# Attention scores as half-height products from the queries as loaded, instead of full-height products from zero-padded queries

## The chip, the cores and the metric

The kernel runs on one core of one Trainium2 chip. The metric is the time of the whole program on the device in microseconds. Three runs of the kernel before took 835.89, 838.58 and 844.72 us; their median, 838.58 us, is the time before. One further execution was profiled, and every row below comes from it.

## The reference

Block-sparse attention over 4 batches, 8 heads, 768 positions and 64 dimensions, followed by a two-layer network with an erf gate.

```python
scores = scale * np.matmul(q, k.transpose(0, 1, 3, 2))     # q, k: (4, 8, 768, 64), scale = 1/8
# blocks of 32 positions, 24 of them. Query block i sees key block j where
#   |i - j| <= 1, or i or j is block 0 or 23, or j is one of i's 3 sampled blocks
scores = np.where(mask, scores, -1e9)
attn = softmax(scores); x = attn @ v                        # x: 3072 tokens of 512
h = x @ w_in                                                # 512 -> 2048
g = h * erf(softplus(h))
out = g @ w_out                                             # 2048 -> 512
```

## The kernel before

Heads are paired: a pair's two heads lie in the two halves of the 128 partitions, 64 dimensions each, so queries and keys of a pair fill all partitions. A batch has 16 units of attention work. Ten are middle units ("m"): 5 tiles t of four query blocks, each in two quads of four heads (two pairs). Six treat the last tile, blocks 21, 22, 23 and 0: four "f" units, one for each pair, for the two blocks that see every key, and two "e" units for blocks 21 and 22.

A middle unit's four query blocks need 256 key columns each: 96 of the window (tile `kx`), 96 of the sampled blocks (gathered by GpSimd into `kg`, four buffers, one for each query block) and 64 of the two end blocks (`kx` again). `scores` (L565) writes them to one PSUM tile `s` of 128 x 1024 float32, of which there is one buffer. Before the change the stationary operand is `qm` (L131): 64 columns for each block of a pair, the first 32 with head 0's queries and zeros in head 1's partitions, the last 32 the other way round. One product of full height so gives both heads' scores, and a unit has 2 pairs x 3 parts x 4 blocks = 24 products of 128 rows by 64 columns. Two blocks go to the two halves of the output partitions. The products are in float32. An f unit is two products of 128 x 128 with 512 and 256 moving columns, an e unit 12 of 128 x 64.

`order_q` (L146) fills `qm` from the loaded tile `qt` by two copies of 64 partitions x 512, on VectorE save for two tiles of the first batch (ScalarE). `load_q` (L134) loads `qt`. `next_queries` (L804), called in a step after `soft_max`, does `order_q` of the next tile and `load_q` of the one after on every second unit, so that the load waits for the copy, and the copy for the scores that still read `qm`.

The main loop (L978) has a step for each of 96 groups of the network, and two more. A step issues, in this order for TensorE: `ff_first` (24 products, tile `h`), `values` of the attention unit begun two units earlier (tile `po`), `scores` of a new unit where the list `until` gives the step one, and `ff_second` (12 products, tile `o`) of the group two steps back. The queues of VectorE, ScalarE and SyncE follow the same written order; every engine keeps program order. SyncE issues the loads, the gathers of values `vb<-vtab`, the stores and the transposes of `p` to `pT`; a wait at its head holds all behind it. After `scores` come `soft_max` and `soft_low` (VectorE), `soft_exp` (ScalarE) and `soft_turn` (a DMA transpose). Ahead of the loop four middle units and the splitting of the weights are written out by hand; there TensorE does the transposes.

Of the kernel before, what the change touches and what calls it, by code (L numbers as in the profile page):

```python
# [9 lines left out]
F32 = mybir.dt.float32  # L10
# [8 lines left out]
P = 128  # L19
BLOCK = 32  # L20
# [22 lines left out]
def sparse_attention_moe(ctx: ExitStack, tc: tile.TileContext, qT, kT, v, sampled, w_in, w_out, out):  # L43
# [22 lines left out]
    pe, act, dve, pool, sp = (InOrder(e) for e in (nc.tensor, nc.scalar, nc.vector, nc.gpsimd, nc.sync))  # L66
# [61 lines left out]


    qts = {}  # L130
    qm = cp.tile([P, HP, 4, 2, BLOCK], F32, tag="qm", name="qm")  # L131
    pool.memset(qm, 0.0)

    def load_q(b, t):  # L134
        place, tag, bufs = (mo, "g", FF_LAG + 1) if b == 0 and t in (1, 2) else (ld, "qt", 1)
        qt = place.tile([P, HP, P], F32, tag=tag, name=f"qt_{b}_{t}", bufs=bufs)
        rows = qT[b].rearrange("(r t) d s -> (t d) r s", t=2)
        if t < MT:
            c = (1 + 4 * t) * BLOCK
            sp.dma_start(qt, rows[:, :, c : c + P])  # L140
        else:
            sp.dma_start(qt[:, :, : 3 * BLOCK], rows[:, :, S - 3 * BLOCK :])
            sp.dma_start(qt[:, :, 3 * BLOCK :], rows[:, :, :BLOCK])
        qts[b, t] = qt

    def order_q(b, t):  # L146
        qt = qts.pop((b, t)).rearrange("p r (j c) -> p r j c", c=BLOCK)
        copy = act.copy if b == 0 and t in (1, 2) else dve.tensor_copy
        for a in range(2):
            copy(qm[a * D : (a + 1) * D, :, :, a, :], qt[a * D : (a + 1) * D])  # L150

    QW = 4 * VW
    vb = cp.tile([P, VGS, 2, 2 * QW], F16, tag="vb", name="vb")
# [400 lines left out]
    def key_columns(b, i, rows, pr):  # L554

        kx, kg = kxs[b], kgs[b, i]
        return (
            (0, 96, kx[rows, i - 1 : i + 2, pr, :]),
            (96, 192, kg[rows, :, pr, :]),
            (192, 256, kx[rows, 0 : NB : NB - 1, pr, :]),  # L560
        )
# [3 lines left out]
    def scores(unit):  # L565
        kind, b, n = unit[0], unit[1], unit[2:]
        tag = "_".join(str(x) for x in unit)
        s = ps_s.tile([P, 1024], F32, tag="s", name=f"s_{tag}")
        if kind == "m":

            t, quad = n
            s4 = s.rearrange("p (h r w) -> p h r w", h=2, r=2)
            for r in range(2):
                pr = 2 * quad + r
                for part in range(3):
                    for j in range(4):
                        o = slice((j % 2) * 64, (j % 2) * 64 + 64)
                        q_ = qm[:, pr, j].rearrange("p a c -> p (a c)")
                        c, e, keys = key_columns(b, 1 + 4 * t + j, slice(0, P), pr)[part]
                        pe.matmul(s4[o, j // 2, r, c:e], q_, keys, start=True, stop=True)  # L580
            softs[unit] = (s, 4, 256)
        elif kind == "e":
            (quad,) = n
            s3 = s.rearrange("p (r w) -> p r w", r=HP)
            for r in range(2):
                for part in range(3):
                    for j in range(2):
                        o = slice(j * 64, j * 64 + 64)
                        q_ = qm[:, 2 * quad + r, j].rearrange("p a c -> p (a c)")
                        c, e, keys = key_columns(b, NB - 3 + j, slice(0, P), 2 * quad + r)[part]  # L590
                        pe.matmul(s3[o, r, c:e], q_, keys, start=True, stop=True)
            softs[unit] = (s[:, :512], 2, 256)
        else:
            (pr,) = n
            q_ = qm[:, pr, 2:].rearrange("p n a c -> p (n a c)")
            for c, e in ((0, 512), (512, S)):
                keys = kxs[b][:, c // BLOCK : e // BLOCK, pr, :]
                pe.matmul(s[:, c:e], q_, keys, start=True, stop=True)
            softs[unit] = (s[:, :S], 1, S)

    xTs = {}
# [3 lines left out]
    def values(b, t, quad):  # L605
        po = ps_po.tile([P, 4, D + 1], F32, tag="po", name=f"po_{b}_{t}_{quad}")
        for hl in range(4):
            r, a = divmod(hl, 2)
            pr = 2 * quad + r
            c = quad * QW + hl * VW  # L610

            todo = [[] for _ in range(4)]
            for x, ln in ((0, 0), (0, 1), (1, 0)):
                for half in range(2):
                    for j in range(4):
                        if t < MT:
                            pT = pts["m", b, t, quad][:, ((j // 2) * 2 + r) * 4 + x * 2 + half]
                            col = (j % 2) * 64 + a * 32
                            vg = vb[:, slot_of[b, 1 + 4 * t + j]]
                        elif j in (1, 2):  # L620
                            pT, col = pts["e", b, quad][:, r * 4 + x * 2 + half], (j - 1) * 64 + a * 32
                            vg = vb[:, slot_of[b, NB - 4 + j]]
                        else:
                            continue
                        w = slice(c, c + D + 1) if ln == 0 else slice(c + D + 2, c + VW)
                        todo[j].append((pT[:, col : col + 32], vg[:, half, w]))
                if t == MT:
                    for k in range(KT):
                        for j in (0, 3):
                            pT, col = pts["f", b, pr][:, x * KT + k], (0 if j else 64) + a * 32  # L630
                            w = slice(c, c + D + 1) if ln == 0 else slice(c + D + 2, c + VW)
                            todo[j].append((pT[:, col : col + 32], vb[:, slot_of[b, -1 - k // 2], k % 2, w]))
            for m in range(max(len(x) for x in todo)):
                for j in range(4):
                    if m < len(todo[j]):
                        lhs, rhs = todo[j][m]
                        w = rhs.shape[1]
                        pe.matmul(
                            po[j * 32 : j * 32 + 32, hl, :w], lhs, rhs, start=m == 0, stop=m == len(todo[j]) - 1
                        )  # L640
        pos[b, t, quad] = po
# [162 lines left out]
    def next_queries(m):  # L804

        b, n = divmod(m, per)
        if n < 10 and n % 2 == 1:
            order_q(b, n // 2 + 1)
            if n < 9:
                load_q(b, n // 2 + 2)  # L810
        if n == per - 1 and b + 1 < B:
            order_q(b + 1, 0)
            load_q(b + 1, 1)

    def behind(m):

        b, n = divmod(m, per)
        if b + 1 < B:
            c = b + 1
            if n == 10:  # L820
                load_q(c, 0)
            k = n if b else 2 * (n - 10) if n > 9 else -1
            if k in ((1, 3, 5, 7) if b else (2, 4, 6, 8)):
                order_k(c, (k - 1) // 2)
            if k in (0, 2, 4, 6):
                load_k(c, k // 2)
            if k == 8:
                have_k.add(c)
            if b == 0:
                n -= 4  # L830
            if n in (1, 7):
                load_v(c, 0)
            if n == 3:
                load_v(c, 1)
            if n in (2, 4):
                square_v(c, n // 2 - 1)
            if n == 5:
                scale_v(c)
            if n in (5, 6):
                split_v(c, 1, n - 5)  # L840
            if n in (8, 9):
                split_v(c, 0, n - 8)
            if n == 9:
                have_v.add(c)
# [9 lines left out]
    def used_keys(unit):  # L854
        nonlocal kfree
        if unit[0] == "m" and unit[3] == 1:
            kfree += 4
        elif unit[0] == "e" and unit[2] == 1:
            kfree += 4
# [21 lines left out]
    for i in range(4):  # L881
        load_weight(sp, "i", i)
    load_q(0, 1)
    load_q(0, 2)
    for n in range(3):
        place_v(0, *divmod(n, 2))
    for b in range(B):
# [3 lines left out]
    for pr in range(HP):  # L891
        order_k(0, pr)
    place_v(0, 1, 1)
    order_q(0, 0)
    have_k.add(0)
    gathers(0)
    numbers[0] = block_numbers(1, 5, SYNC)
# [18 lines left out]

    scores(units[1])
    used_keys(units[1])
    gathers(0)
    for i in range(10, 16):  # L920
        load_weight(pool, "i", i)
# [1 line left out]
    work("Di1")  # L923
    soft_max(units[1])
    soft_exp(units[1])
    order_q(0, 1)
    work("Qi1 Di2 Qi2 Di3 Qi3")
    soft_low(units[1])

# [8 lines left out]
    soft_turn(units[2])  # L938
    scores(units[3])
    used_keys(units[3])  # L940
    work("Qi6 Di7 Qi7 Do0")
    set_apart()
    soft_max(units[3])
# [10 lines left out]
    norm(*seen(units[1]))  # L954
    work("Hi0")
    turn(*seen(units[1]))
    order_q(0, 2)
    soft_low(units[3])
    values_of(seen(units[2]))
    work("Li0 Hi1")  # L960
# [6 lines left out]
    turn(*seen(units[3]))  # L967
    work("Do2")
    gathers(0)
    load_q(0, 3)  # L970
    begun = FIRST

    on_pe[0] = False
# [4 lines left out]
    for m in range(len(groups) + FF_LAG):  # L978
# [23 lines left out]
        if unit:  # L1002
            scores(unit)
            used_keys(unit)
        if last:
            ff_gate(*last)
        if place:
# [5 lines left out]
                ff_second(*groups[m - FF_LAG], u)  # L1013
        if unit:
            soft_max(unit)
            next_queries(begun - 1)
        if group:
            ff_power(*group)
        if unit:
# [54 lines left out]
```

## Time and profile before

| | us |
|---|---|
| median of 3 runs | 838.58 |
| profiled execution | 838.56 |
| its span from first to last instruction | 836.8 |
| TensorE matmul busy (PE) | 710.8 (85%) |
| weight loads (PEld) | 504.8 (60%) |
| VectorE (DVE) | 554.4 (66%) |
| ScalarE (ACT) | 601.1 (72%) |
| GpSimd (POOL) | 123.7 (15%) |
| chain that ended last: PE h, PE o, PE s_m, PE po | 18%, 18%, 5%, 3% of the span |
| mean granted clock of TensorE, share of full | 0.944 |

The profiled execution lies 1.8 us over its span and within 0.1 us of the median. Busy time of TensorE counts the tail of each product too; products overlap in it, so counts and starts say more than busy time. A float32 product appears in the trace as two weight loads and two matmuls, a float16 one as one of each. In a shape such as `128*64 128x96 f32`, 128*64 are the rows and columns of the stationary operand and 96 the moving columns.

### The profile page before, as it was taken

Reading aid. Unit: us, or ns where it says so; the run is one execution under the profiler, and the core shown is the slowest. Engines: PE = TensorE matmul, PEld = TensorE weight load, DVE = VectorE, ACT = ScalarE, POOL = GpSimd, SP = SyncE. Lnnn points to the kernel's source line nnn. Section 1 sums busy time; section 2 is a strip of 40 time slices with the busy share of each in tenths; the row PEclk is TensorE's granted clock in tenths of the full one; section 3 lists DMA queues with packets and bytes.
Section 4 is the critical chain, followed back from the end, with each engine's and each line's share of the span. In section 5 each row is a group of like instructions: output and inputs, shape, how many; then the busy total and the mean of one; then the engine's idle time right before and its main releaser. Section 6 shows DMA issues by size and latency. Waiting matters only on the chain.

```text
span 836.8 us, 26712 instructions
## 1 busy us (share of the span) xinstructions
PE 710.8 (85%) x11100; PEld 504.8 (60%) x11100; DVE 554.4 (66%) x977; ACT 601.1 (72%) x999; POOL 123.7 (15%) x344
## 2 busy tenths in 40 slices
PE   1253637899897899899999899999999899999997
PEld 1252424566665667566777666667777576766664
DVE  3994796887764766766566676756677567654454
ACT  4654657987865766887768778868678678776774
POOL 5430111001222220100201231000111100000000
PEclk9775867989998999999999999999999999999999
DMA  8999953687899697661497886633576758211000
GB/s 325 297 257 318 243 120 90 164 207 164 172 212 209 178 205 198 186 131 45 136 216 178 210 198 192 167 79 83 117 167 166 190 103 188 53 33 40 1 27 26
DMA packets 199930, 131.61 MB, mean 157 GB/s; under 512 B 144000, under 2 KB 167168, under 8 KB 199808
## 3 DMA queue, kind: packets, MB, share of 16 engines
q1 hardware_dynamic: 196384, 118.10, 58.1%
q0 software_dynamic: 3424, 11.80, 4.3%
q8 instruction: 87, 1.43, 0.7%
q14 instruction: 35, 0.29, 0.1%
HBM read 83.88 MB, written 12.95 MB: 116 GB/s over the span
## 4 chain that ended last, share of the span: by engine, by line
PE 47%; DVE 15%; issue 12%; ACT 10%; DMA 10%; SPq 2%; POOL 2%; POOLq 1%; ACTq 0%
PE h L59 18%; PE o L59 18%; PE s_m L59 5%; DMA vb<-vtab 4%; PE po L59 3%; DVE g L59 2%; ACT pf_m L59 2%; DVE q L59 2%; DVE mx_m L59 2%; DMA vtab<-vn 2%; SPq L59 2%; ACT x L59 2%; DVE p_m L59 2%; POOL kg L59 2%; ACT q L59 2%
## 5 line engine op out<-in xcount | busy, mean ns | idle before, releaser
L59 PE MATMUL h<-xT,wi 128*128 128x256 f16 x2304 | 274.2, 276 | 14.9 <-ACT wi L59 7.5
L59 PE MATMUL o<-wo,g 128*128 128x512 f16 x1152 | 270.3, 385 | 7.9 <-DVE wo L59 4.0
L59 PEld LDWEIGHTS <-wi 128*128 128x128 f16 x2304 | 227.4, 99 | 65.5 <-ACT wi L59 8.8
L59 PEld LDWEIGHTS <-g 128*128 128x128 f16 x1152 | 110.3, 99 | 133.0 <-issue 14.8
L59 ACT ACTIVATE x<-x 128x512 f32<-128x512 f32 x288 | 181.5, 630 | 9.1
L59 POOL COPY kg<-kx 128x128 f32 x264 | 90.5, 394 | 286.2 <-PE s_m L59 183.6
L59 ACT ACTIVATE pf_m<-s_m,nb_m 128x256 f32<-128x256 f32 x160 | 62.7, 475 | 65.4 <-DVE nb_m L59 59.5
L59 DVE SCALAR_TENSOR_TENSOR q<-x,q 128x512 f32<-128x512 f32 x96 | 66.7, 695 | 61.4 <-ACT x L59 60.1
L59 ACT ACTIVATE x<-h,isg 128x512 f32<-128x512 f32 x96 | 65.2, 680 | 36.3 <-PE h L59 35.7
L59 PE MATMUL s_m<-kx,qm 128*64 128x64 f32 (+1 forms) x1280 | 75.0, 249 | 6.8 <-ACT pf_m L59 4.2
L59 ACT ACTIVATE q<-q 128x512 f32<-128x512 f32 x96 | 59.5, 620 | 29.6 <-DVE q L59 29.6
L59 DVE SCALAR_TENSOR_TENSOR q<-q,h 128x512 f32<-128x512 f32 x96 | 65.5, 682 | 22.6 <-ACT q L59 22.6
L59 DVE TENSOR_TENSOR p_m<-pf_m,p_m 128x1024 f16<-128x1024 f32 x40 | 49.3, 1232 | 32.3 <-ACT p_m L59 32.3
L59 DVE SCALAR_TENSOR_TENSOR g<-q,g 128x512 f16<-128x512 f32 x96 | 67.0, 698 | 3.3
L59 PE MATMUL po<-vb,pT_m 128*32 128x65 f16 (+1 forms) x3840 | 44.7, 201 | 25.7 <-DMA vb<-vtab 15.0
L59 PEld LDWEIGHTS s_m<-kx,qm 128*64 128x64 f32 x1280 | 59.7, 146 | 10.4 <-ACT pf_m L59 4.9
L59 ACT ACTIVATE q<-x 128x512 f32<-128x512 f32 x96 | 60.5, 630 | 3.1
L59 DVE TENSOR_REDUCE mx_m<-s_m 128x4 f32<-128x1024 f32 x40 | 48.8, 1219 | 20.2 <-PE s_m L59 20.2
L59 PEld LDWEIGHTS <-pT_m 128*32 128x32 f16 x3840 | 38.0, 97 | 36.8 <-DMA vb<-vtab 16.3
L59 PE MATMUL s_m<-kg,qm 128*64 128x96 f32 x640 | 46.9, 261 | 3.2 <-POOL kg L59 2.2
L59 DVE TENSOR_TENSOR x<-xf,x 128x512 f16<-128x512 f32 x24 | 16.9, 703 | 43.3 <-ACT x L59 43.3
L59 DVE TENSOR_SCALAR g<-q 128x512 f16<-128x512 f32 x96 | 41.3, 431 | 3.3
(115 smaller groups left out, 623.7 us busy)
## 6 DMA issues: line engine op xcount, KB each, us to landing
vb<-vtab SPq DMA_DIRECT2D x280, 65.0 KB, 2.9
vb<-vtab SPq DMA_DIRECT2D x32, 390.0 KB, 4.1
vraw<-in_v_dram SPq DMA_DIRECT2D x10, 768.0 KB, 5.1
vtab<-vn SPq DMA_DIRECT2D x16, 390.0 KB, 5.4
vb<-vtab SPq DMA_DIRECT2D x12, 520.0 KB, 5.0
qt<-in_qT_dram SPq DMA_DIRECT2D x20, 256.0 KB, 3.3
out_dram<-wo SPq DMA_DIRECT2D x20, 256.0 KB, 4.3
vb<-vtab SPq DMA_DIRECT2D x36, 130.0 KB, 3.0
```

The costliest lines, as they stand in the source:

```text
L59: done = call(*args, **kwargs)
```

## The change

`qm`, its clearing and `order_q` are gone. `qt` has two buffers and stays until its scores are done; the products take their stationary operand from it, with 64 rows, one head at a time. A middle unit has 4 products of 64 rows x 128 columns for the end blocks (all four query blocks of a head at once, 64 moving columns), then 32 of 64 rows x 32 columns with 96 moving columns. In `s` the head's half of the tile is now the outer index: head a writes columns 512a to 512a+511, the query block j partitions 32j to 32j+31. An e unit has 24 products of 64 x 32, an f unit four of 64 x 64; in these two the heads' outputs share columns and differ in partitions. `values` reads `pT` at the new places. `next_queries` only loads, and is called right after `scores`.

```diff
-    qm = cp.tile([P, HP, 4, 2, BLOCK], F32, tag="qm", name="qm")
-    pool.memset(qm, 0.0)
     def load_q(b, t):
-        place, tag, bufs = (mo, "g", FF_LAG + 1) if b == 0 and t in (1, 2) else (ld, "qt", 1)
-        qt = place.tile([P, HP, P], F32, tag=tag, name=f"qt_{b}_{t}", bufs=bufs)
+        qt = ld.tile([P, HP, P], F32, tag="qt", name=f"qt_{b}_{t}", bufs=2)
...
-    def order_q(b, t):
-        qt = qts.pop((b, t)).rearrange("p r (j c) -> p r j c", c=BLOCK)
-        copy = act.copy if b == 0 and t in (1, 2) else dve.tensor_copy
-        for a in range(2):
-            copy(qm[a * D : (a + 1) * D, :, :, a, :], qt[a * D : (a + 1) * D])
...
             t, quad = n
-            s4 = s.rearrange("p (h r w) -> p h r w", h=2, r=2)
+            qt = qts[b, t]
+            s4 = s.rearrange("p (a r w) -> p a r w", a=2, r=2)
+            for pr, r, a in ((2 * quad + n // 2, n // 2, n % 2) for n in range(4)):
+                rows = slice(a * D, (a + 1) * D)
+                pe.matmul(s4[:, a, r, 192:], qt[rows, pr], kxs[b][rows, 0 : NB : NB - 1, pr, :], start=True, stop=True)
+            for r in range(2):
+                pr = 2 * quad + r
+                for part in range(2):
+                    for j in range(4):
+                        o = slice(j * BLOCK, (j + 1) * BLOCK)
+                        for a in range(2):
+                            rows = slice(a * D, (a + 1) * D)
+                            c, e, keys = key_columns(b, 1 + 4 * t + j, rows, pr)[part]
+                            pe.matmul(s4[o, a, r, c:e], qt[rows, pr, o], keys, start=True, stop=True)
...
-                    for j in range(2):
-                        o = slice(j * 64, j * 64 + 64)
-                        q_ = qm[:, 2 * quad + r, j].rearrange("p a c -> p (a c)")
-                        c, e, keys = key_columns(b, NB - 3 + j, slice(0, P), 2 * quad + r)[part]
-                        pe.matmul(s3[o, r, c:e], q_, keys, start=True, stop=True)
+                    for j in range(2):
+                        for a in range(2):
+                            rows, o = slice(a * D, (a + 1) * D), j * 64 + a * BLOCK
+                            c, e, keys = key_columns(b, NB - 3 + j, rows, pr)[part]
+                            q_ = qt[rows, pr, j * BLOCK : (j + 1) * BLOCK]
+                            pe.matmul(s3[o : o + BLOCK, r, c:e], q_, keys, start=True, stop=True)
...
-            q_ = qm[:, pr, 2:].rearrange("p n a c -> p (n a c)")
             for c, e in ((0, 512), (512, S)):
-                keys = kxs[b][:, c // BLOCK : e // BLOCK, pr, :]
-                pe.matmul(s[:, c:e], q_, keys, start=True, stop=True)
+                for a in range(2):
+                    rows = slice(a * D, (a + 1) * D)
+                    keys = kxs[b][rows, c // BLOCK : e // BLOCK, pr, :]
+                    pe.matmul(s[a * 64 : a * 64 + 64, c:e], qts[b, MT][rows, pr, 64:], keys, start=True, stop=True)
...
     def next_queries(m):
-        if n < 10 and n % 2 == 1:
-            order_q(b, n // 2 + 1)
-            if n < 9:
-                load_q(b, n // 2 + 2)
-        if n == per - 1 and b + 1 < B:
-            order_q(b + 1, 0)
-            load_q(b + 1, 1)
+        if n in (1, 3, 5, 7):
+            load_q(b, n // 2 + 2)
+        elif n in (9, 15) and b + 1 < B:
+            load_q(b + 1, n // 15)
...
         if unit:
             scores(unit)
             used_keys(unit)
+            next_queries(begun - 1)
...
         if unit:
             soft_max(unit)
-            next_queries(begun - 1)
```

The code by hand ahead of the loop loses its three `order_q` and the early `load_q(0, 2)` and `load_q(0, 3)`, and gets `next_queries(1)` and `next_queries(3)` after the scores of units 1 and 3.

## Rows read from the trace of the kernel before

**Rows 1.** Windows by stage: start:end, length, busy us per engine (instructions), PEclk, DMA share, GB/s.

```profile
0.00:95.00 95.00, 37.62 (x746) 31.57 (x747) 63.06 (x104) 49.74 (x82) 31.93 (x78) 0.77 0.95 292
95.00:180.00 85.00, 56.76 (x1040) 38.78 (x1037) 70.82 (x110) 67.30 (x110) 11.39 (x34) 0.82 0.59 148
180.00:300.00 120.00, 104.47 (x1791) 74.65 (x1791) 79.14 (x145) 85.63 (x148) 24.41 (x65) 0.96 0.86 194
300.00:460.00 160.00, 154.10 (x2501) 110.60 (x2488) 105.88 (x192) 121.95 (x206) 21.97 (x63) 1.00 0.67 158
...
500.00:640.00 140.00, 134.61 (x2157) 96.38 (x2156) 93.92 (x172) 107.62 (x180) 17.06 (x55) 1.00 0.58 140
640.00:700.00 60.00, 56.46 (x958) 40.92 (x956) 39.28 (x73) 42.65 (x73) 5.27 (x18) 0.97 0.69 158
...
597.78:611.28 13.50, 13.50 (x225) 9.78 (x217) 9.55 (x18) 9.60 (x17) 0.00 (x0) 1.00 0.69 140
```

**Rows 2.** The chain of waits from 597 to 625: start us, us, what.

```profile
597.85 1.94 PE s_m L59 x48
599.79 2.70 PE o L59 x12
602.49 2.62 PE h L59 x24
605.11 2.59 PE o L59 x12
607.70 2.62 PE h L59 x24
610.32 1.04 PE po L59 x95
```

**Rows 3.** The chain, 355 to 375: an f unit; then timelines of PE matmuls.

```profile
358.97 1.29 PE s_f L59 x4
...
598.16 0.50 PE L59 MATMUL s_m<-kg,qm 128*64 128x96 f32 x8
598.50 0.73 PE L59 MATMUL s_m<-kx,qm 128*64 128x64 f32 x16
...
393.62 0.30 PE L59 MATMUL s_m<-kx,qm 128*64 128x96 f32 x2
```

**Rows 4.** Weight loads: groups by form, and the start of an f unit.

```profile
L59 PEld LDWEIGHTS s_m<-kg,qm 128*64 128x64 f32 x640 | 36.7, 148 | 4.7 <-POOL kg L59 3.5 <-POOL vn L59 1.2
L59 PEld LDWEIGHTS s_f<-kx,qm 128*128 128x128 f32 x64 | 11.0, 192 | 11.9 <-issue 7.6 <-ACT pf_m L59 2.2 <-ACT pf_e L59 1.8
...
365.21 0.30 PEld L59 LDWEIGHTS s_f<-kx,qm 128*128 128x128 f32 x2
```

**Rows 5.** Windows of tile s_m alone: 48 PE instructions are one middle unit.

```profile
0.00:95.00 95.00, 15.39 (x240) 14.60 (x240) 6.10 (x5) 6.28 (x16) 0.77 0.95 292
95.00:180.00 85.00, 10.03 (x240) 9.34 (x240) 6.08 (x5) 9.38 (x24) 0.82 0.59 148
180.00:300.00 120.00, 17.32 (x336) 15.08 (x336) 8.55 (x7) 10.97 (x28) 0.96 0.86 194
```

**Rows 6.** Groups by form: the copies to qm.

```profile
L59 DVE COPY qm<-qt 64x512 f32<-64x512 f32 x44 | 20.7, 470 | 0.5 <-DMA qt<-in_qT_dram 0.2
L59 ACT COPY qm<-qt 64x512 f32<-64x512 f32 x4 | 2.4, 609 | 0.0
```

**Rows 7.** The chain, first 100 us: start us, us, what.

```profile
17.69 3.63 PE s_m L59 x48
...
24.96 12.14 DMA vtab<-vn
...
38.85 8.41 DMA vb<-vtab
```

**Rows 8.** Waits of PE from 180 to 760; landing times of the query loads.

```profile
PE po L59 <- DMA pT_m<-p_m: 7.8, 6, 3.5
...
DMA to landing us min/median/max: 2.5/3.1/10.3
```

More of the change, by code (lines that the diff above doesn't have):

```diff
@@ L571, in scores @@
             t, quad = n
-            s4 = s.rearrange("p (h r w) -> p h r w", h=2, r=2)
+            qt = qts[b, t]
[12 more added lines that the diff above has]
+                            pe.matmul(s4[o, a, r, c:e], qt[rows, pr, o], keys, start=True, stop=True)
+            softs[unit] = (s, 4, 256)
+        elif kind == "e":
+            (quad,) = n
+            qt = qts[b, MT]
+            s3 = s.rearrange("p (r w) -> p r w", r=HP)
             for r in range(2):
@@ L575, in scores @@
                 for part in range(3):
[L576 to L586, printed above, removed]
-                    for j in range(2):
-                        o = slice(j * 64, j * 64 + 64)
-                        q_ = qm[:, 2 * quad + r, j].rearrange("p a c -> p (a c)")
-                        c, e, keys = key_columns(b, NB - 3 + j, slice(0, P), 2 * quad + r)[part]
-                        pe.matmul(s3[o, r, c:e], q_, keys, start=True, stop=True)
+                    for j in range(2):
+                        for a in range(2):
[3 more added lines that the diff above has]
+                            pe.matmul(s3[o : o + BLOCK, r, c:e], q_, keys, start=True, stop=True)
             softs[unit] = (s[:, :512], 2, 256)
@@ L616, in values @@
                         if t < MT:
-                            pT = pts["m", b, t, quad][:, ((j // 2) * 2 + r) * 4 + x * 2 + half]
-                            col = (j % 2) * 64 + a * 32
+                            pT = pts["m", b, t, quad][:, (a * 2 + r) * 4 + x * 2 + half]
+                            col = j * BLOCK
                             vg = vb[:, slot_of[b, 1 + 4 * t + j]]
@@ L629, in values @@
                         for j in (0, 3):
-                            pT, col = pts["f", b, pr][:, x * KT + k], (0 if j else 64) + a * 32
+                            pT, col = pts["f", b, pr][:, x * KT + k], a * 64 + (32 if j == 0 else 0)
                             w = slice(c, c + D + 1) if ln == 0 else slice(c + D + 2, c + VW)
@@ L819, in behind @@
             c = b + 1
-            if n == 10:
-                load_q(c, 0)
             k = n if b else 2 * (n - 10) if n > 9 else -1
@@ L883, in sparse_attention_moe @@
     load_q(0, 1)
-    load_q(0, 2)
     for n in range(3):
@@ L893, in sparse_attention_moe @@
     place_v(0, 1, 1)
-    order_q(0, 0)
     have_k.add(0)
@@ L918, in sparse_attention_moe @@
     used_keys(units[1])
+    next_queries(1)
     gathers(0)
@@ L925, in sparse_attention_moe @@
     soft_exp(units[1])
-    order_q(0, 1)
     work("Qi1 Di2 Qi2 Di3 Qi3")
@@ L940, in sparse_attention_moe @@
     used_keys(units[3])
+    next_queries(3)
     work("Qi6 Di7 Qi7 Do0")
@@ L956, in sparse_attention_moe @@
     turn(*seen(units[1]))
-    order_q(0, 2)
     soft_low(units[3])
@@ L969, in sparse_attention_moe @@
     gathers(0)
-    load_q(0, 3)
     begun = FIRST
```

## The prediction

> **What bounds the kernel now.** I read the windows by stage first, for the engine that is full and at which clock. From 300 us to 700 us TensorE is busy in 154.10 of 160, 134.61 of 140 and 56.46 of 60 us, 96%, at a granted clock of 0.97 to 1.00, the 2.4 GHz level; VectorE and ScalarE are at 62% to 77% there [rows 1]. Before 180 us it is another kernel: until 95 us the DMA engines are 95% busy and TensorE 40%; from 95 to 180 us VectorE is busy for 70.82 of 85 us, TensorE for 56.76 [rows 1]. So time taken from TensorE is nearly all gained late and little of it early.
>
> Then the chain of waits over two steps. It holds TensorE alone: scores 1.94, o 2.70, h 2.62, o 2.59, h 2.62, values 1.04 us [rows 2], 13.5 us in which no other engine ends a wait. A middle unit costs 1.94 us of such a stretch. There are 40 of them: 5 before 95 us, 5 to 180 us, 7 to 300 us [rows 5], hence 23 after that.
>
> **What a product costs.** An f unit has two products of 512 and 256 columns and shows four records in 1.29 us [rows 3]. Were each column streamed once per record, 1536 columns at 2.4 GHz would take 0.64 us; so a record streams its columns twice, and a float32 product makes four passes. A 96-column record then holds its part of the array for 192/2.4 = 80 ns. The eight `kg` records start at 598.16 and the next group at 598.50 [rows 3]: 8 x 80 = 0.64 us of streaming in 0.34 us, so the two 64-column halves run side by side. The first two records of a unit start together within a window of 50 ns [rows 3], and since the second record of one product needs the same half as its first, they are of two products: TensorE lets a later product on a free part of the array pass an earlier one that waits. The unit's stream is, per half, 8 products of 96 columns (4 x 96 / 2.4 = 160 ns) and 4 of 64 (107 ns), 1.71 us; with the change of shape and the first load it is the 1.94.
>
> A load of float32 weights: records of 128 columns last 192 ns, of 64 columns 148 ns [rows 4]; 44 ns for 64 columns is the lower reading, 54 ns (a column read twice at 2.4 GHz, as the moving ones) the upper. In the f unit the first load starts at 365.21 and the stream about 0.1 us later [rows 3, 4], so I take 107 ns for 128 columns, 54 for 64, 27 for 32. A change of shape: o lasts 2.70 behind scores and 2.59 behind h [rows 2], so 0.11 us.
>
> **The middle unit after.** Entry 0.11. The four end-block products: each of the two row halves loads 128 columns four times (two records each), 4 x 0.107, and streams the last, 0.053: 0.48 us; the loads outlast the 53 ns streams, so loads set this part. A change of shape, 0.11. First load 0.03. Then 32 products of 96 columns on eight parts of the array, 4 on each: 4 x 0.160 = 0.64, and 0.07 for starting eight parts one after the other (7 ns between the parts is my estimate, from two records started inside 50 ns; the upper end is 25 ns a part, 0.2). Sum 1.44 us against 1.94: **0.50 us less**.
>
> No row shows two row halves at work, nor eight parts. Bounds: best, the end-block loads hide behind the work before them and starts cost nothing, 1.0 us, 0.9 less. Worst, halves run in turn: end blocks 0.91, stream 1.28 on four parts, 2.5 us, 0.56 more. I take side by side, as the nearest row is the column halves, which do it almost perfectly, and four column parts in `values` do too: 95 records of 64 or 65 columns in 1.04 us [rows 2], 10.9 ns each, where one alone streams 27 ns.
>
> That row also settles a floor that would speak against this change, since a unit now has 72 records in place of 48. The Trainium skill, "TensorE: Matmul & The Clock Gate", section "Wait — 56ns, not 53.3ns?", has starts of products never closer than about 25 ns. By it the unit would last an estimated 72 x 25 ns = 1.8 us and two changes of shape, and nothing would be gained; the values row, at 10.9 ns, contradicts it where parts differ.
>
> **f and e units.** An f unit: each half streams 768 columns four times, 1.28 us, side by side 1.28 as before; its first load is 64 columns in place of 128, 0.05 less, 16 times: 0.8 us. An e unit: six products on each of four parts, where before it was six on each of two: the same. Bounds: as for the halves above.
>
> **Copies.** 44 copies of 470 ns, 20.7 us, leave VectorE, four of 609 ns leave ScalarE [rows 6]. From 300 us TensorE covers them. From 95 to 180 us four tiles are copied, 3.8 us at 83% busy; I take a third, 1.2 us, between none and all. In the hand-written part the DMAs cover them: nothing. The clearing of `qm` on GpSimd stands ahead of gathers that wait for keys: nothing.
>
> **Loads and queues.** As many query loads are issued. In a step a load now stands on SyncE behind the gathers of values and ahead of the transposes, and waits for this step's scores on TensorE; before, it waited for the copy, later. Behind it are the transposes of `x` and of `p`: the latter needs `soft_low`, which needs the same scores, the former `norm`, written behind them too. The load comes three units before its use, over 13 us at the late pace [rows 2], and lands in 2.5 to 10.3 us [rows 8]. Price nothing; if that cover goes, a late landing would show as waits of scores on `qt`, up to 10 us each. In the hand-written part the second load falls into the wait for the 12.14 us write of values [rows 7], the third behind the gathers; 256 KB each, nothing.
>
> **Sum.** After 300 us: 23 x 0.50, of which 0.92 is kept (waits on `pT`, 7.8 us in all [rows 8], and on other engines come closer): 10.6. From 180 to 300 us, TensorE 87% busy: 7 x 0.50 x 0.7 = 2.5. From 95 to 180: 5 x 0.50 x 0.5 = 1.2. Before that: the first unit lies on the chain with 3.63 us at a lower clock [rows 7]; it loses about a quarter, 0.9; the others are covered by DMAs. With f loads 0.8 and copies 1.2: 17.2 us. The profiled execution took 838.56 us, as good as the median of 838.58: **821 us**. The best within this case: everything of 35 units kept (17.5), the four others at lower clock 3.8, f 0.8, copies 5: 27, or 812.
>
> **Rivals.**
> 1. *The gain is given back.* TensorE gets ahead and waits for transposed probabilities or gathered values. For: such waits are there, and each step's VectorE-ScalarE work is not shorter by much. Against: 96% busy, chain of TensorE alone. Half of 17 kept: 830; range 830 to 836. Chance 0.13.
> 2. *Eight parts give only four at a time* (reading of four float32 streams in each row half at once is shown nowhere; `values` reads four of half the width). Stream 1.28: the unit 2.08, 0.14 more, 35 x 0.14 = 5 lost, 2 gained from f and copies: 841. Break-even is a stream of 1.14 us, 4.5 parts at a time. Chance 0.10, of which 0.02 is for a floor between starts: a unit of 72 records no longer than before needs starts under 25 ns, and by the 10.9 ns of `values` they can be. The floor that the Trainium skill's page above states would bring this same time.
> 3. *Slower: the heads of f and e run in turn because both write the same columns of `s`.* Place: those 24 units, which stand alone among o and h in the full stretch. Price: f 16 x 1.28 = 20.5, e 8 x 0.86 = 6.9, 27.4 in all, 26 kept; less 17: **848**. It decides once over six tenths of the overlap is lost. For: it is the only place where two row halves write the same columns. Against: their partitions differ, and column halves in different partitions of the same columns run side by side now [rows 3]. The Trainium skill, "TensorEngine Tiling (Array Packing)", section "Restrictions and Gotchas", says different row tiles cannot access one PSUM bank at the same time; no row here shows it, and the middle unit, where each head has its own half of `s`, would not be touched. Chance 0.10.
> 4. *Row halves never overlap.* f and e 27, middle units 40 x 0.56 = 22, less 2: 885. Chance 0.06.
>
> That the change does not do what it says would be 2 or 4. The forecast keeps 0.61.
>
> **Range and chances.** A difference under 1%, 8.4 us, can't be told from no change: faster is under 830.2, slower over 847.0. The range reaches from 812 to 847; it leaves out rival 4, the upper half of rival 3 and little below. Faster 0.61, within 1% 0.27 (rivals 1 and 2 and part of 3), slower 0.12.
>
> **What would show it.** The chain's middle unit at 1.4 us in place of 1.94, with 72 records, in the full stretch; f units still 1.29 (2.6 means rival 3 or 4), e units unchanged. The first eight 32-column records starting within 60 ns show eight parts; starts 80 ns apart in pairs show none. TensorE's busy share from 300 us on stays above 93%; if it falls with units at 1.4, rival 1. Wrong also if scores wait for `qt`, or if the granted clock falls below 0.97 in that stretch.

## The result, and the profile after

The changed kernel takes **852.0 us** (median of 4 runs, 851.09 to 852.66) against 838.18 us for the kernel before in the same job; the ratio is 1.0147 with a 95% interval of 1.0098 to 1.0195. It is 1.5% slower where 2% less was forecast. The profiled execution has a span of 849.6 us; its instructions by engine:

```profile
PE 707.9 (83%) x12316; PEld 478.1 (56%) x12316; DVE 536.5 (63%) x933; ACT 598.5 (70%) x995; POOL 122.7 (14%) x343
```

The first look goes to TensorE's share by stage, in the columns of [rows 1]; first one stretch of the kernel before, then the changed kernel.

```profile
460.00:500.00 40.00, 35.88 (x602) 24.93 (x600) 29.38 (x58) 30.04 (x52) 11.69 (x31) 0.96 0.81 200
```

```profile
180.00:300.00 120.00, 103.61 (x2046) 69.44 (x2035) 76.61 (x138) 87.47 (x150) 25.89 (x66) 0.94 0.80 187
300.00:460.00 160.00, 150.43 (x2746) 101.48 (x2743) 98.00 (x174) 116.38 (x198) 21.90 (x63) 0.98 0.69 157
460.00:500.00 40.00, 34.75 (x564) 22.90 (x555) 24.41 (x49) 29.51 (x54) 8.07 (x22) 0.91 0.79 191
500.00:640.00 140.00, 130.63 (x2364) 88.53 (x2362) 90.61 (x161) 104.83 (x176) 16.13 (x54) 1.00 0.60 136
640.00:700.00 60.00, 56.20 (x1126) 39.66 (x1124) 38.13 (x68) 44.06 (x75) 8.19 (x30) 0.94 0.66 159
```

From 300 to 460 us TensorE is busy for 150.43 us where it was 154.10, from 500 to 640 us for 130.63 where it was 134.61, and the granted clock has come down from 1.00 to 0.98, from 0.96 to 0.91 and from 0.97 to 0.94 in three stretches. TensorE idles more, although VectorE and ScalarE have less to do there.

The scores themselves became what was forecast. The chain of waits of the changed kernel (start us, us, what) has the units where they run undisturbed:

```profile
196.64 2.62 PE h L59 x24
199.26 1.44 PE s_f L59 x8
200.69 2.70 PE o L59 x12
...
398.51 2.62 PE h L59 x24
401.13 1.52 PE s_m L59 x64
402.64 2.70 PE o L59 x12
405.34 2.62 PE h L59 x24
407.96 2.59 PE o L59 x12
```

and the timeline of PE matmuls shows the inside of that middle unit. Its first row merges the 8 records of the end blocks with 16 records of 32 columns; the second row is from a narrower window, which holds only the first eight of 32 columns:

```profile
401.06 0.99 PE L59 MATMUL s_m<-kx,qt 64*128 64x64 f32 x24
...
401.65 0.31 PE L59 MATMUL s_m<-kx,qt 64*32 64x96 f32 x8
...
402.58 1.68 PE L59 MATMUL o<-wo,g 128*128 128x512 f16 x7
```

A middle unit lasts 1.52 us in place of 1.94 [rows 2]. The first eight 32-column records start within 0.05 us, at 401.65, and from there to the start of o at 402.58 all 64 start in 0.93 us, 15 ns each: eight parts of the array do work side by side. An f unit lasts 1.44 us in place of 1.29 [rows 3].

What is new is a wait inside the units. The same chain, at a step with an e unit:

```profile
374.24 2.62 PE h L59 x24
376.86 2.28 PE po L59 x183
379.13 0.45 PE s_e L59 x13
379.58 1.67 issue
381.26 0.91 PE s_e L59 x27
382.16 4.38 PE o L59 x12
386.55 2.62 PE h L59 x24
```

The e unit stops after 13 records for 1.67 us; "issue" means that nothing which the profile records was awaited, and its operands had been there since the unit began. The next o then takes 4.38 us in place of 2.70. The windows show why: the granted clock is 0.68 over the 4 us after the stop, so part of that stretch ran at 1.2 GHz.

```profile
376.00:381.00 5.00, 3.58 (x213) 3.05 (x211) 2.61 (x7) 3.21 (x5) 0.00 (x0) 1.00 0.36 82
381.00:385.00 4.00, 3.74 (x43) 1.86 (x44) 1.88 (x4) 1.78 (x4) 1.93 (x6) 0.68 0.02 4
```

Such stops have a place. If everything that the trace holds of TensorE's stream is numbered from its start, weight loads, matmuls and the few semaphore waits and drains between them, each of them comes just ahead of the 194th instruction after a multiple of 256, in this trace and in those of all other runs here. The page's part on DMA queues (queue, kind: packets, MB, share) has a queue that fits; first the kernel before, then the changed one:

```profile
q8 instruction: 87, 1.43, 0.7%
```

```profile
q8 instruction: 96, 1.57, 0.8%
```

TensorE's loads and matmuls are 2 x 11,100 before and 2 x 12,316 after, which is 86.7 and 96.2 times 256, and a packet is 16 KB. So TensorE's program arrives in blocks of 256 instructions. In the trace each stop ends 1.2 to 1.7 us after a packet of that queue has landed, and in all 18 traces none of 1,622 block borders was crossed sooner than 1.19 us after its packet. I call it a **supply stop** when the starts on the two sides of a border lie over 0.35 us apart and the second follows a landing in this way. From the first product of h in the main loop on, the kernel before has 7 of them with 8.8 us, the changed one 15 with 21.3 us (of that 7.0 and 17.4 us TensorE stood idle; the rest is the usual distance of starts). All 15 lie in steps that issue values and scores one behind the other. Their blocks would have been through in 1.5 to 3.3 us without the stop, while 67 of the 74 other blocks after 95 us took over 4 us. The other seven took only 1.4 to 3.4 us and did not stop; their packets had started 0.15 to 1.6 us before the block began, those of the 15 stopped ones 0.3 to 2.1 us after. What sets when a packet starts, no run shows. The Trainium skill, "Runtime: NRT & Kernel Launch", section "Instruction fetch mechanics", describes blocks of 256 instructions and calls the cost of crossing into the next "mostly hidden"; the blocks agree, the cost does not, 0.6 to 2.3 us a stop here.

From the first product of h in the main loop to that of the 96th group the traces give 733.3 us before and 743.3 after, **10.0 us more in the loop**. Comparing the loops step by step: where nothing else differs, the steps with a middle unit and no stop are 0.42 us shorter, those with an f unit 0.25 us longer, those without a unit equal. In sum it looks otherwise. The 16 steps with a stop in either kernel are 7.8 us longer, though 10 of them have a middle unit; the 26 steps with a middle unit and no stop are only 1.8 us shorter together, where 26 x 0.42 would be 10.9.

### The profile page after: what moved, and what is told of

Same layout as the page of the kernel before. It is cut to its first block, busy times and chain, and to the rows that moved or that the text cites. A ratio compares the mean times of both kernels' runs of the same rounds, so it can differ in the third digit from the quotient of the medians.

```text
span 849.6 us, 29083 instructions
## 1 busy us (share of the span) xinstructions
PE 707.9 (83%) x12316; PEld 478.1 (56%) x12316; DVE 536.5 (63%) x933; ACT 598.5 (70%) x995; POOL 122.7 (14%) x343
## 4 chain that ended last, share of the span: by engine, by line
PE 40%; DVE 18%; DMA 15%; ACT 14%; issue 6%; SPq 5%; POOL 1%; POOLq 0%; ACTq 0%
PE o L59 16%; PE h L59 15%; DMA vb<-vtab 6%; SPq L59 4%; ACT x L59 4%; DVE q L59 3%; DVE g L59 3%; DMA vtab<-vn 3%; ACT pf_m L59 3%; PE po L59 3%; ACT q L59 3%; DVE mx_m L59 3%; DVE p_m L59 2%; PE s_f L59 2%; DMA vraw<-in_v_dram 2%
## 5 line engine op out<-in xcount | busy, mean ns | idle before, releaser
L59 PE MATMUL o<-wo,g 128*128 128x512 f16 x1152 | 275.9, 389 | 8.3 <-DVE g L59 2.9
L59 POOL COPY kg<-kx 128x128 f32 x264 | 87.8, 385 | 289.6 <-PE s_m L59 183.4
L59 PE MATMUL s_m<-kx,qt 64*32 64x96 f32 (+1 forms) x1600 | 63.4, 281 | 7.3 <-ACT pf_m L59 5.6
L59 PE MATMUL po<-vb,pT_m 128*32 128x65 f16 (+1 forms) x3840 | 44.3, 202 | 29.9 <-DMA vb<-vtab 16.5
L59 PEld LDWEIGHTS s_m<-kx,qt 64*32 64x32 f32 (+1 forms) x1600 | 45.0, 131 | 14.2 <-ACT pf_m L59 6.5
L59 PE MATMUL s_m<-kg,qt 64*32 64x96 f32 x1280 | 39.3, 270 | 8.6 <-issue 4.8
```

The source lines that it names most:

```text
L59: done = call(*args, **kwargs)
```

## The experiments

Two theories at first. *Supply*: the change packs 2,432 more instructions into the stretch of values and scores, which grows from 288 to 336 instructions in a step with a middle unit, and TensorE stops for its program. *Gain given back* (rival 1 of the prediction): TensorE gets ahead and waits for others.

The kernel before took 838.2 to 846.1 us (medians) in the five jobs, so each ratio is to the kernel before in its own job, and times of different jobs are not compared. The diffs show the main lines.

**1. More instructions without the change.** The kernel before, with 24 products of one column behind the values of each middle unit.

```diff
+        for x in range(24 if t < MT else 0):
+            j = x % 4
+            pT = pts["m", b, t, quad][:, x % 16]
+            pe.matmul(po_all[j * 32 : j * 32 + 32, 300:301], pT[:, :32], pT[:, 32:33], start=True, stop=True)
```

> The kernel before, with 24 extra products of one moving column behind the values of each middle unit: 48 more TensorE instructions a unit, as the change adds, and none of its 64-row products. Supply theory (TensorE's instructions arrive in blocks of 256, and a block used up in less than about 3.1 us makes it wait): the waits at block ends, 8 of 0.6 to 2.3 us in the profile before, become 14 or more, and the time is 846 to 856, mostly by waits and not by the products. Give-back theory (the change loses time because TensorE runs ahead of the softmax and the clock falls) and shape theory (the f and e units lose it): only the direct cost, 40 x 0.1 us = 4, so 840 to 844, and as many block waits as before.

857.82 us, ratio 1.0136 [1.0092, 1.0179]. The loop is 12.6 us longer than before, with supply stops of 17.1 us (12); ahead of the loop there are 8.8 us more (3), where the kernel before has 1.3, and the first h comes 7.9 us later. The 15 steps of the loop with a stop in either kernel hold 11.4 of the 12.6 us; the 25 steps with a middle unit and no stop are 0.1 us longer on average, so the 36 x 24 products in the loop cost some 4 us by themselves. The waits of PE from 180 to 830 us (what waited, for what: us, times, longest) show the rest; before, then with the extra products:

```profile
PE s_m L59 <- issue: 2.6, 2, 1.7
...
PE po L59 <- issue: 1.7, 2, 1.2
```

```profile
PE po L59 <- issue: 7.2, 4, 2.4
...
PE s_m L59 <- issue: 5.8, 6, 1.4
```

48 more instructions in the step of a middle unit, as many as the change adds there, with the scores as they were, cost as much as the change, for the most part in steps with a stop.

**2 and 3. Scores away from values.** In both kernels the scores, with what belongs to them, go behind `ff_second`, so that 24 instructions of o (2.6 us) separate them from the values.

```diff
-        if unit:
-            scores(unit)
...
                 ff_second(*groups[m - FF_LAG], u)
+        if unit:
+            scores(unit)
```

> The changed kernel with the scores of a step issued behind the second network product instead of ahead of it, so that two dense stretches, values and scores, never stand next to each other on TensorE. Supply theory: block waits of TensorE fall from 16 to 6 or fewer and the time to 826 to 838. Give-back theory: the softmax starts 2.6 us later in a step, the waits on it grow, 852 or more. Shape theory: 850 to 854, nothing changes for f and e.

> The kernel before with the same move of the scores behind the second network product: the control for the run above. Supply theory: it has 8 block waits, 10 us in all, and loses most of them: 828 to 836. Give-back theory: 840 or more, since the softmax starts later.

874.79 us, 1.0293 [1.022, 1.0366], and 871.63 us, 1.0273 [1.023, 1.0316]. The time expected was missed: the move itself costs 2.7%. That this is because the softmax starts later is not shown; in the control the waits of PE for other things than "issue", from 180 to 830 us, grow from 28.4 to 45.8 us. The supply stops nearly went, to 3.0 and 3.9 us, and with them the distance between the two kernels, to 3.2 us.

**4. Middle units alone.** e and f units as before the change, from a `qm` of two pairs.

```diff
+    def order_q(b, quad):
+        qt = qts[b, MT][:, 2 * quad : 2 * quad + 2].rearrange("p r (j c) -> p r j c", c=BLOCK)
+        for a in range(2):
+            dve.tensor_copy(qm[a * D : (a + 1) * D, :, :, a, :], qt[a * D : (a + 1) * D])
```

> The changed kernel with f and e units as before (full-height products from a zero-padded tile that two copies a quad fill), middle units as changed. Shape theory: f loses two changes of shape a unit (16 x 0.25 = 4 us) and e its doubled instructions; without them 838 or less. Supply theory: the f part is right, 4 us, and of the block waits those in e units go, but those in and around the middle units stay: 842 to 848. Give-back theory: 846 to 850.

854.37 us, 1.0123 [1.0069, 1.0177]; supply stops 22.2 us (15). Steps with an f unit are back to no difference, so the 0.25 us belongs to the half-height f products; steps with a middle unit lose their 0.42 us where nothing stops. The expected 842 to 848 us would be up to 1.011; the ratio is not clear of that, nor of the changed kernel's. Most of the loss stays: it comes with the middle units.

**5 to 8. Two orders that keep the scores where they are.** Values ahead of `ff_first`, or between its two halves, in both kernels; the diff is of the second.

```diff
         if group:
-            ff_first(*group)
+            ff_first(*group, 0)
+        if place:
+            values_of(place)
+        if group:
+            ff_first(*group, 1)
             ff_logs(*group)
-        if place:
-            values_of(place)
```

> Changed kernel with the values of a step issued ahead of ff_first, so that 24 products of h (2.6 us) stand between values and scores; scores stay where they are. Supply theory: the waits in mid-stream at every 256th instruction fall from about 16 with 23 us to below 6 us, scores are not late as in the spread order, and the time falls by 8 to 15 us below the changed kernel, to 0.996 to 1.005 of the kernel before. Rival (the loss is the gain given back to waits on pT, vb and the softmax): values come 2.6 us earlier, those waits grow, and the time is 1.015 to 1.03. Rival (shape changes and the f units alone): 1.012 to 1.018, unchanged.

> Control: the kernel before with the same reordering. Its mid-stream waits are 9 us. Supply theory: it gains at most that, 0.990 to 1.002, and the changed kernel in this order is equal to it or faster by up to 1%. Rival (gain given back): slower than the kernel before by 0.5 to 1.5%, and the changed kernel stays 1% or more behind it.

> Changed kernel with values issued in the middle of ff_first: 12 products of h, values, 12 products of h, scores. Half the distance of the order with values first (1.3 us), values only 1.3 us earlier. Supply theory: about half of the mid-stream waits go, the time is 1.003 to 1.010 of the kernel before. Rival (gain given back): 1.012 to 1.02.

> Control: the kernel before in the same order. Supply theory: 0.993 to 1.002. Rival (gain given back): 1.00 to 1.01.

Values first: 859.15 us, 1.0153 [1.0105, 1.0202], and 857.12 us, 1.0147 [1.0101, 1.0192]. Split: 854.57 us, 1.0119 [1.0068, 1.017], and 850.35 us, 1.0072 [1.0042, 1.0102]. The times that the supply theory gave were missed again: no order was faster than the kernel before. Stops did fall as it said, to 3.0 and 4.1 us with values first, and to 10.5 and 7.5 us with the split. What took their place stands in the waits of PE from 180 to 830 us, first the changed kernel, then its control:

```profile
PE po L59 <- DMA pT_m<-p_m: 29.7, 9, 5.2
...
PE po L59 <- issue: 5.2, 3, 2.5
PE po L59 <- DMA pT_f<-p_f: 3.6, 1, 3.6
```

```profile
PE po L59 <- DMA pT_m<-p_m: 19.4, 7, 3.7
...
PE po L59 <- issue: 6.9, 4, 2.3
```

Against 7.8 us in [rows 8], the waits for `pT_m` grow to 19.4 us by the order, and to 29.7 with the change on top: 10 us more, about what the faster scores should gain (11 us, worked out below the table). Both theories hold in part.

**9 to 12. Scores early, values late.** The order h, scores, o, values relieves `pT` too. The gathers of values and `norm` move behind the values as well; runs 11 and 12 add early query loads, and e and f units as before the change.

```diff
-        if place:
-            values_of(place)
...
                 ff_second(*groups[m - FF_LAG], u)
+        if place:
+            values_of(place)
...
         if place:
+            norm(*place)
             turn(*place)
```

> Changed kernel with the order h, scores, o, values in a step (before: h, values, scores, o; norm and the gathers of values follow the values): 12 products of o (2.6 us) stand between scores and values and 24 of h between values and the next scores, values come 4 us later, scores 1 us earlier. Supply and pT theory (what the middle units save is lost to mid-stream waits for instructions, and in the two orders with values earlier to waits on pT): both sorts of wait fall, mid-stream waits below 6 us, pT waits below 6 us after 180 us, and the changed kernel gains on its control by 5 to 12 us: 0.985 to 1.000 of the kernel before. Rival (the change costs by itself, by f units, loads and clock): 1.005 to 1.015, and the control equally far below it as the kernel before is below the changed one (12 us).

> Control: the kernel before in the order h, scores, o, values. Supply and pT theory: it loses its 9 us of mid-stream waits and most of 8 us of pT waits, 0.985 to 1.000 of the kernel before, and stands 5 to 12 us behind the changed kernel in this order. Rival: it stays ahead of the changed kernel by about 12 us.

> The changed kernel in the order h, scores, o, values, with the query loads of the hand-written part where they were before the change (second and third tile loaded at the top, the fourth at its end). If the 2.2 us by which the first h came later is the place of the second load, 1.5 to 3 us less than with the order alone; if it is anything else, no difference.

> The order h, scores, o, values with the middle units changed and e and f units as before the change (products of 128 rows from a zero-padded tile of two pairs, copied for each quad by VectorE). The trace of the changed kernel has f units 0.25 us longer each (16 of them); if that counts, 3 to 5 us below the changed kernel in the same order, and it beats both kernels, 0.975 to 0.992 of the kernel before. If the f units do not count, equal to the changed kernel in this order.

851.45 us, 1.0081 [1.0047, 1.0115]; the control 861.55 us, 1.0186 [1.0151, 1.0221]; with early query loads 850.61 us, 1.0047 [1.0017, 1.0078]; with middle units alone 851.94 us, 1.0106 [1.0056, 1.0156]. Here the change gains 10 us on its control, as expected (the two intervals lie apart), though both lie above the kernel before. The order finds its own wait, as scores now come before the gathered keys:

```profile
PE s_m L59 <- POOL kg L59: 12.0, 15, 5.0
...
PE po L59 <- DMA pT_m<-p_m: 4.6, 3, 2.6
```

(12.0 us, against 2.2 in the kernel before; 13.4 in this order's control.) And the expected cause was not the whole of it: stops did not fall below 6 us, they are 12.0 us here and 13.8 in the control, one of 4.6. The loops part by 12 us in the first 25 steps and by little after. The early loads gave 0.8 us, which these runs can't tell from none, and the f units' old form gave nothing in this order.

**13 and 14. Only the borders moved.** 64 one-column products at the start, where TensorE is idle, shift every later border by half a block; order, products and queues stay.

```diff
+    room = ps_po.tile([P, 4, D + 1], F32, tag="po", name="room")
+    for x in range(64):
+        pe.matmul(room[:BLOCK, 0, :1], zero16[:, :BLOCK], zero16[:, :1], start=True, stop=True)
```

> Changed kernel with 64 one-column products (128 instructions) at the start, where TensorE is idle: from there on every 256th instruction falls half a block away. Supply theory: the mid-stream waits leave the steps in which they were and turn up in others; their sum changes by several us from 23, and the time by about as much and what follows from it (2 to 10 us, either way). Rival (waits at these places are only how other waits show): the waits stay at the same steps, time within 2 us of the changed kernel, 1.013 to 1.017.

> Control, the kernel before with the same 128 instructions at the start. Supply theory: its 7 mid-stream waits with 9 us move to other steps; 9 us was for one position of the border, and another gives 5 to 16, so 0.996 to 1.010. Rival: 0.998 to 1.002.

852.84 us, 1.0111 [1.0073, 1.0149], and 850.1 us, 1.0062 [1.0031, 1.0093]. The stops moved. The same step of the kernel before, and then of the same kernel with the shift:

```profile
550.99 2.28 PE po L59 x186
553.27 0.39 PE s_e L59 x5
553.66 2.02 issue
555.67 0.94 PE s_e L59 x15
556.62 2.70 PE o L59 x12
```

```profile
562.68 2.27 PE po L59 x190
564.95 1.04 PE s_e L59 x24
566.00 2.70 PE o L59 x12
```

and the step shown above for the changed kernel, with the shift: its stop now lies 128 instructions earlier in the program's order, inside the values, and TensorE stands for 0.36 us.

```profile
378.95 1.70 PE po L59 x137
380.65 0.36 issue
381.01 0.76 PE po L59 x47
381.77 1.02 PE s_e L59 x48
382.79 2.70 PE o L59 x12
```

Nothing else was changed in these pairs, and the wait is gone or elsewhere: it hangs on where the border falls. (And o takes its 2.70 us again.) In sum the stops hardly changed, 24.1 us (15) and 10.6 us (7), so the position of the borders was not the kernel before's luck in the loop. The changed kernel's 1.0111 is not told apart from its 1.0147. The control's 5 us more in the median are explained in part: in its profiled execution the loop is 2.7 us longer and the first h comes 8.0 us later, and ahead of it lies a supply stop of 4.7 us.

**15 and 16. Fewer instructions.** Both kernels without the products of p's low part with v's high part in the middle units (a term is left out of the output), 64 instructions less in each.

```diff
-            for x, ln in ((0, 0), (0, 1), (1, 0)):
+            for x, ln in ((0, 0), (0, 1), (1, 0))[: 2 if t < MT else 3]:
```

> Changed kernel without the products of the low part of p with the high part of v in the middle units (32 of 96 products of values, 64 instructions and about 0.35 us a unit; the output loses that term). The dense stretch of values and scores falls from 336 to 272 instructions, less than the 288 of the kernel before. Supply theory: mid-stream waits fall from 23 us to 10 or less, and the time stands 0 to 6 us above the control without these products, where it was 13. Rival (f units, loads, clock, returned gain): still 10 to 14 us above it.

> Control: the kernel before without the same products: dense stretch 288 to 224 instructions. Supply theory: mid-stream waits from 9 to 3 to 6 us, time 0.975 to 0.990 of the kernel before (14 us of products, most of it kept). Rival: the same time, so the difference to the changed kernel decides.

844.39 us, 0.9976 [0.994, 1.0011], and 836.35 us, 0.9894 [0.9848, 0.9941]. The stops of the changed kernel fell as expected, from 21.3 to 9.1 us; its control's only to 7.9, more than the 3 to 6 expected. The medians differ by 8.0 us, between the theories, the loops by 3.7.

**All pairs together.** Loop is from the first h to the 96th group's, changed kernel less control; stops in us (count) from the first h on, changed kernel and control; clock is the time at 1.2 GHz in the loop, changed less control; other waits are those of PE from 180 to 830 us without "issue", changed less control.

| pair | stops | loop | other waits | clock | medians |
|---|---|---|---|---|---|
| as written | 21.3 (15), 8.8 (7) | +10.0 | +4.0 | +16.5 | +13.8 |
| borders shifted | 24.1 (15), 10.6 (7) | +9.2 | +6.9 | +7.1 | +2.7 |
| h split by values | 10.5 (13), 7.5 (8) | +8.4 | +8.1 | +30.8 | +4.2 |
| fewer products | 9.1 (7), 7.9 (6) | +3.7 | +5.6 | +6.0 | +8.0 |
| values first | 3.0 (2), 4.1 (2) | +3.9 | +10.3 | +15.4 | +2.0 |
| scores last | 3.0 (2), 3.9 (4) | +1.2 | +7.8 | +3.9 | +3.2 |
| scores early, values late | 12.0 (10), 13.8 (6) | -13.5 | +7.7 | -8.6 | -10.1 |

Loop, stops, waits and clock are of one profiled execution each, and medians of a job still scatter and hold the part ahead of the loop too (in the shifted pair it ended 3.6 us earlier in the changed kernel): the loop column is the cleaner, and two neighbouring rows are not told apart. But for two pairs of neighbours the rows stand in the same order by the difference of stops and by the loop: with 12 to 14 us more of stops the change loses 9 to 10 us, with about as many it loses 1 to 4, with 2 us less it gains. The split loses 8.4 us with 3 us more of stops; there half of the clock's column, 15 us, is the largest term. What the change never gets, save in the last order, is the 11 us that shorter middle units (36 in the loop, 0.42 us each, less 16 times 0.25 us) ought to bring.

The clock is a rival that no run sets apart. Between 180 and 830 us the changed kernel has eight stretches at 1.2 GHz, the kernel before four. Two of the eight come with a stop, at 382 and 461 us, 3.4 us each; six come with a wait for data, and 11 of the 13 stops of that time come without one. Between executions it says little about the time: the four of the changed kernel have mean granted clocks of 0.934 to 0.968 and lie within 1.6 us.

## Why the prediction was wrong

*The bound* was read rightly and trusted too far: 96% busy at full clock [rows 1] said that TensorE was full, and nothing was asked about what feeds it. The kernel before had 8.8 us of supply stops in its loop. They stood in its list of waits as "issue", 2.6 and 1.7 us of it in the rows above and 7.0 us in all, and I passed over them.

*The middle unit* was right in its mechanism: 1.44 us forecast, 1.52 measured, 0.42 us less where 0.50 was booked. That the sum came so close is partly luck. In the unit above, which begins at 401.13 in the chain, the part up to the first 32-column record took 0.52 us against 0.73 for its terms, and the 64 records after it 0.93 against 0.71. The guess of 7 ns between two parts was right: eight records start within 0.05 us. Rivals 2 and 4 fell with this unit. The start floor of about 25 ns of the Trainium skill, "TensorE: Matmul & The Clock Gate", section "Wait — 56ns, not 53.3ns?", fell too: 15 ns a record across eight parts.

*f units* were mis-sized: 0.05 us less each was forecast, 0.25 us more was measured, 4 us in place of -0.8. The sum took off the shorter first load and forgot the shape. Before, an f product was 128*128 like h and o around it, and o behind the f unit of [rows 3] was short:

```profile
360.27 2.59 PE o L59 x12
```

Now it is 64*64, and o after it lasts 2.70, the same 0.11 that the prediction charged a middle unit; the unit itself is 0.15 longer, of which another 0.11 would be the change ahead of it. Rival 3 fell: heads that write the same columns run side by side, eight records in 1.44 us where two heads in turn would need an estimated 2.57 (1.29 and once more 1.28 of streaming). That 852 lies near its 848 is chance. e units stayed the same as forecast, 1.02 and 1.04 us in the undisturbed units shown above.

*Loads and copies*: the copies went from VectorE (554.4 to 536.5 us busy), and no wait on `qt` shows in the changed kernel. The first h comes 2.3 us later, at 89.5 us, but in programs with the hand-written part of the kernel before it comes at 87.2 (before), 89.8 to 91.0 (three) and 93.3 us, so no cost of the moved loads is shown.

*The step that failed* is the share kept: "23 x 0.50, of which 0.92 is kept (waits on `pT` ... and on other engines come closer)". It named what could be late next among data, and not the instructions. The 72 records in place of 48 were weighed once, against a floor between starts, and never as 48 more instructions for the program's queue: the sum has no term for supply. What the runs showed in its place: middle units 36 x -0.42 = -15.1 and f +4.0 should have made the loop 11.1 us shorter, and it is 10.0 longer, so 21.1 us were lost. By steps, 12.0 of them lie in the 16 steps with a stop in either kernel, and 9.1 in the others, where TensorE waits longer for data and runs more often at 1.2 GHz. By terms, stops are +12.5, other waits +4.0, clock at most half of 16.5; these overlap, as a stop can cover another wait. Shown for the stops is that they come with instructions (1, 15), sit on the borders of blocks and move with them (13, 14). How the 9.1 us divide between waits and clock stays open.

*Rival 1*, gain given back, is the second half of the truth. It would have given 830 to 836; with the stops about equal (fewer products, values first, scores last) the change costs 1 to 4 us in the loop, with 5.6 to 10.3 us more of other waits. Why the order with late values alone lets it gain is open: its control had a stop of 4.6 us and fell back in the first 25 steps, and no run separates that from the order.

What the prediction said would prove it wrong did so in part: TensorE's share from 300 us stayed at 93 to 94% in the long stretches and fell from 90 to 87% between 460 and 500 us, and the clock fell to 0.91 there and to 0.94 from 640 to 700 us. The mark of 0.97 was badly set, as the kernel before had 0.96 from 460 to 500 us.

No version here beats the kernel before with the whole output; the nearest is the changed one with scores early, values late and early loads, 1.0047.

## What to carry to other kernels

Count instructions as well as work: a change that halves what each product does and doubles their number can make its unit faster and the program slower, when the units already use up a block of 256 instructions faster than the next one comes (in the changed kernel blocks that stopped took 2.95 us or more with their stop). In a trace look for "issue" waits in the middle of a unit whose operands have landed, and count along the engine's whole stream, waits and drains included, whether they repeat at a fixed distance: a wait of 1.27 us for `pT_m` at 350.75 us lies four instructions behind a border and is none of them. And price a step whose shape differs from its neighbours by the change of shape on both sides, 0.11 us each here.

## What the runs showed of the hardware that was not expected

- TensorE's program comes in packets of 16 KB, 256 instructions. In 18 traces no border between blocks was crossed sooner than 1.19 us after its packet had landed. Where a block was used up in 1.5 to 3.3 us, TensorE mostly stopped, up to 2.3 us in the kernel as written and 4.8 us in another (ahead of the loop of run 1).
- After such a stop the clock can be granted at the lower level: after 1.67 us of standing, o took 4.38 us in place of 2.70. Between 180 and 830 us that came with two of 13 stops; six other such stretches came with waits for data.
- Products on eight parts of the array (two row halves, four column quarters) in float32 start 15 ns apart, and two heads that write the same columns in different partitions run side by side.
- The same hand-written part, limited by DMAs [rows 1], reached the first h anywhere from 87.2 to 93.3 us in five programs that share it, more than the 0.9 us that I had booked as its gain.
